# Decay factors of a gated linear attention by in-place products instead of summed logarithms, gates and angles with tokens on the partitions

## The chip, the cores and the metric

The kernel runs on one core of a Trainium2 chip. TensorE (PE) multiplies matrices, VectorE (DVE) and ScalarE (ACT) work element by element, GpSimd (POOL) does little here, and SyncE (SP) issues the loads. Each engine works through its own instructions in order. The metric is the device time of one execution in microseconds (us), the median of several runs. Everything is float32; a float32 matmul shows as two PE instructions in the profile, a float32 transpose as one.

## The reference

The first half is a gated linear attention: batch 4, 8 heads, 768 tokens, 48 channels a head, with a complex gate per token and channel. The second half is a mixer over tokens (rank 32) and a two-layer MLP (384 to 1536 to 384).

```python
mag = np.sqrt(a_re * a_re + a_im * a_im)
scale = np.minimum(mag, 0.999) / (mag + 1e-06)
a_re_n, a_im_n = (a_re * scale, a_im * scale)
for t in range(S):
    ar, ai = (a_re_n[:, :, t, :, None], a_im_n[:, :, t, :, None])
    new_re = ar * S_re - ai * S_im
    new_im = ar * S_im + ai * S_re
    kv = np.einsum('bhd,bhe->bhde', k[:, :, t], v[:, :, t])
    S_re, S_im = (new_re + kv, new_im)
    y[:, :, t] = np.einsum('bhd,bhde->bhe', q[:, :, t], S_re)
...
xt = x.transpose(0, 2, 1)          # x: y as (batch, token, head*channel)
h = xt @ U @ V
u = x + h.transpose(0, 2, 1)
ch = np.maximum(u @ w_ch1, 0.0) @ w_ch2
return (u + ch).astype(np.float32)
```

## The kernel before

The 3072 tokens are 24 chunks of 128, six to a batch. Within a chunk, y_t sums q_t k_s times a decay between s and t times the cosine of an angle difference times v_s. Cosine and sine of the summed angles are stacked, so that a head's q and k have 96 rows (48 cosines, 48 sines). The pairs (s, t) of a chunk are cut into seven levels: halves of 64, 32, 16, 8, 4, 2 and 1 tokens, in which s lies in the lower half of a block and t in the upper; one more pass takes s = t.

For each chunk `front_steps` turns q and k to channels on partitions (`turned`, L275) and multiplies them with cosine and sine while they leave PSUM (L277). `decays` sums the logarithms of the gate magnitudes over every token's span by a matmul with a 0/1 matrix of 384 columns, three levels (or suffix and prefix) for one head at a time: 24 such matmuls a chunk (L300), each followed by an exp on ACT into the tile W (L302, shown by the profile as L182, the line of the helper `act`). `weigh` multiplies W by q or k (L311). `own` and `back_steps` then make the products of k and q: 32-token blocks for the inner levels (`blocks`, L286; 32 matmuls a level in four column tiles), merged by masks into the tile DG (L280); `corners` (L364) and `corner` (L356) for the two outer levels. `place` copies DG to the diagonal of AT on POOL (L378). `outputs` multiplies AT by v and adds the carried state G (L393, L395); ACT copies the result, tokens on partitions, to x (L397). `keys` and `state` (L386, L402) carry the state on. Every level has its own factors in W, so no level waits for another.

`gate_steps` makes the logarithms and angles, two chunks at a time, with tokens on partitions; `phase` sums the angles per head by a matmul (L255) with channels on partitions, reduces them (L260 to L264) and takes one sine (L266).

`mixer_steps` works on two chunks of the batch before: `rank`, `mixed`, `uT` (L440, L449, L454), 12 steps of `up` (L462) and two of `down` (L470). In the first five slots DVE also rounds the float64 weights (`single`, L159 to L170).

The program is written slot by slot, one chunk's `back_steps` to a slot; `weave` spreads the steps of the streams of a slot evenly: the next chunk's factors, gates, weights and half a mixer call. The framework then schedules the instructions within each engine's queue. Three mixer calls, for the last batch, stand behind the loop.

## Time and profile before

| | |
|---|---|
| time, median of 3 runs | 1436.69 us (1436.44 to 1446.21) |
| profiled execution, first to last instruction | 1440.2 us |
| PE busy | 1286.4 us, 89% |
| DVE busy | 722.3 us, 50% |
| ACT busy | 728.7 us, 51%, of it 227.1 us in 177 loads of function tables |
| POOL busy | 114.5 us, 8% |

The span and the runs agree within 0.3%. A row of the profile names a line, an engine and an operation, the tiles written and read, the shape (partitions x elements) and the count. PEclk is the granted clock of TensorE as a share of full speed. The x copy of L397 is the last step of a chunk's attention and serves as a milestone.

### The profile page before, as it was taken

Reading aid. Unit: us, or ns where it says so; the run is one execution under the profiler, and the core shown is the slowest. Engines: PE = TensorE matmul, PEld = TensorE weight load, DVE = VectorE, ACT = ScalarE, POOL = GpSimd, SP = SyncE. Lnnn points to the kernel's source line nnn. Section 1 sums busy time; section 2 is a strip of 40 time slices with the busy share of each in tenths; the row PEclk is TensorE's granted clock in tenths of the full one; section 3 lists DMA queues with packets and bytes.
Section 4 is the critical chain, followed back from the end, with each engine's and each line's share of the span. In section 5 each row is a group of like instructions: output and inputs, shape, how many; then the busy total and the mean of one; then the engine's idle time right before and its main releaser. Section 6 shows DMA issues by size and latency. Waiting matters only on the chain. (4 is left out here: it accounts for less than half of the span.)

```text
span 1440.2 us, 33570 instructions
## 1 busy us (share of the span) xinstructions
PE 1286.4 (89%) x15080; PEld 849.6 (59%) x15080; DVE 722.3 (50%) x1359; ACT 728.7 (51%) x1205; POOL 114.5 (8%) x130
## 2 busy tenths in 40 slices
PE   3785878668898999998998998998999999999998
PEld 1452554435576666675565675675566576675666
DVE  3787588585665355455255355355265444420000
ACT  7875337246687167277176267368166263230111
POOL 0003110410001000000001000000000000000000
PEclk9997767688898999999999999999899999999999
DMA  7132223130212102102102102101101100000000
GB/s 147 27 68 56 62 66 92 42 86 10 51 29 46 28 18 47 39 7 46 31 15 46 28 19 46 28 19 24 28 18 24 39 7 2 13 2 11 11 11 11
DMA packets 181103, 50.42 MB, mean 35 GB/s; under 512 B 176416, under 2 KB 176544, under 8 KB 180960
## 3 DMA queue, kind: packets, MB, share of 16 engines
q1 hardware_dynamic: 179424, 43.56, 14.2%
q0 software_dynamic: 1536, 4.72, 0.9%
q8 instruction: 118, 1.93, 0.6%
q14 instruction: 25, 0.20, 0.0%
HBM read 43.55 MB, written 4.72 MB: 34 GB/s over the span
## 5 line engine op out<-in xcount | busy, mean ns | idle before, releaser
L300 PE MATMUL e<-span,lm 128*96 128x384 f32 x1152 | 477.9, 530 | 70.2 <-ACT W L182 52.4
L182 ACT ACTIVATE W<-e 96x384 f32<-96x384 f32 x576 | 272.7, 486 | 303.0 <-PE e L300 248.6
L300 PEld LDWEIGHTS e<-span,lm 128*96 128x96 f32 x1152 | 171.3, 172 | 216.1 <-ACT W L182 141.0
L182 ACT ACT_TABLE_LOAD x177 | 227.1, 1283 | 9.1 <-DMA ar<-in_a_re_dram 4.5
L462 PE MATMUL up<-uT,w 128*128 128x256 f32 x864 | 228.8, 405 | 2.6 <-DVE uT L455 1.9
L311 DVE TENSOR_TENSOR W<-W,kT 96x512 f32<-96x512 f32 x192 | 144.7, 754 | 142.7 <-ACT W L182 142.7
L462 PEld LDWEIGHTS up<-uT,w 128*128 128x128 f32 x864 | 166.8, 200 | 42.3 <-issue 10.8
L470 PE MATMUL down<-w,h 128*128 128x384 f32 x576 | 189.0, 486 | 0.0
L378 POOL COPY AT<-DG 32x256 f32<-32x256 f32 x96 | 98.5, 1026 | 888.9 <-DVE DG L280 884.7
L470 PEld LDWEIGHTS down<-w,h 128*128 128x128 f32 x576 | 109.4, 190 | 75.9 <-issue 2.5
L311 DVE TENSOR_TENSOR W<-W,qT 96x512 f32<-96x512 f32 x192 | 144.9, 755 | 1.5 <-ACT W L182 1.1
L182 ACT ACTIVATE h<-up 128x256 f32<-128x256 f32 x144 | 55.1, 382 | 167.9 <-PE up L462 167.4
L473 DVE TENSOR_TENSOR x<-down,x 128x384 f32<-128x384 f32 x24 | 13.4, 557 | 222.5 <-PE down L470 222.5
L286 PEld LDWEIGHTS inner<-W 96*32 96x32 f32 x7680 | 85.2, 113 | 63.7 <-issue 51.6
L393 PE MATMUL y<-v,AT 128*128 128x48 f32 x384 | 79.9, 306 | 35.2 <-POOL AT L378 35.2
L286 PE MATMUL inner<-W 96*32 96x32 f32 x7680 | 102.0, 202 | 7.9 <-issue 6.6
L393 PEld LDWEIGHTS y<-v,AT 128*128 128x128 f32 x384 | 68.9, 226 | 41.2 <-POOL AT L378 36.7
L260 DVE TENSOR_TENSOR f<-ph,last 96x512 f32<-96x512 f32 x40 | 27.4, 684 | 92.9 <-PE ph L255 87.7
L395 PE MATMUL y<-G,W 96*128 96x48 f32 x320 | 72.8, 315 | 0.0
L280 DVE COPY_PREDICATED DG<-mask,inner 128x256 f32<-128x256 int32 x120 | 52.3, 436 | 23.8 <-PE inner L286 22.7
L395 PEld LDWEIGHTS y<-G,W 96*128 96x128 f32 x320 | 61.1, 234 | 2.7 <-issue 1.8
L255 PE MATMUL ph<-span,th 128*96 128x128 f32 x384 | 54.5, 286 | 6.1 <-DVE f L260 4.7
(86 smaller groups left out, 1103.4 us busy)
## 6 DMA issues: line engine op xcount, KB each, us to landing
q<-in_q_dram SPq DMA_DIRECT2D x48, 192.0 KB, 3.2
k<-in_k_dram SPq DMA_DIRECT2D x48, 192.0 KB, 3.8
raw<-in_moe_w_ch_dram SPq DMA_DIRECT2D x24, 384.0 KB, 3.2
ar<-in_a_re_dram SPq DMA_DIRECT2D x24, 192.0 KB, 3.4
ai<-in_a_im_dram SPq DMA_DIRECT2D x24, 192.0 KB, 3.7
v<-in_v_dram SPq DMA_DIRECT2D x24, 192.0 KB, 2.6
out_dram<-x POOLq DMA_DIRECT2D x24, 192.0 KB, 2.1
span<-in_spans_dram SPq DMA_DIRECT2D x1, 576.0 KB, 5.4
```

The lines of the kernel that those rows point to most:

```text
L182: nc.scalar.activation(out=o, in_=i, func=f, **kw)
L255: nc.tensor.matmul(out=ps[0:D2, j], lhsT=head(th, hh * HH + j), rhs=prefix, start=True, stop=True)
L260: nc.vector.tensor_tensor(out=f, in0=ps[0:D2], in1=T["last", i - 1][:, hs].unsqueeze(2).to_broadcast([D2, HH, CH]), op=OP.add)
L280: nc.vector.copy_predicated(out=DG[i % 2], mask=mask[:, n].unsqueeze(1).to_broadcast([128, H, BLK]), data=ps)
L286: nc.tensor.matmul(out=ps[js, h], lhsT=lhs(h)[:, js], rhs=rhs(h)[:, js], start=True, stop=True, tile_position=(0, j * BLK))
L300: nc.tensor.matmul(out=ps[0:D2].rearrange("p l t -> p (l t)"), lhsT=head(lm, h), rhs=span[:, tri * 3 * CH:(tri + 1) * 3 * CH], start=True, ...
L311: nc.vector.tensor_tensor(out=o, in0=o, in1=f, op=OP.mult)
L378: nc.gpsimd.tensor_copy(out=AT[i % 2][js, :, js], in_=DG[i % 2][js])
L393: nc.tensor.matmul(out=y[:, h], lhsT=AT[i % 2][:, h], rhs=T["v", i][:, h], start=True, stop=(c == 0))
L395: nc.tensor.matmul(out=y[:, h], lhsT=w[:, h], rhs=T["G"][:, h], start=False, stop=True)
L462: nc.tensor.matmul(out=ps, lhsT=w1[:, f, ff * 128:(ff + 1) * 128], rhs=st["uT"][:, f], start=(f == 0), stop=(f == KD - 1))
L470: nc.tensor.matmul(out=ps, lhsT=st["h"][:, ff, cc * CH:(cc + 1) * CH], rhs=w2[:, ff], start=(ff == 0), stop=(ff == KF - 1))
```

## The change

The decays are no longer sums of logarithms. `gate_steps`, now for three chunks at a time, makes the gate magnitude m itself, the decay from each token to its chunk's end (suf, by one matmul of 384 columns a chunk) and cosine and sine, all with tokens on the partitions: the angles are summed by one or two matmuls a chunk (prefix, and tail for the chunk before). `prep_steps` multiplies q and k with cosine and sine, then turns q, k and m to channels on partitions (`turn`: 24 transposes, six ACT copies from PSUM), and forms the products of m over blocks of 2, 4, ... 128 tokens (`totals`, seven products on DVE). `chain_steps` keeps one pair of factors q, k (tile QK) and grows it in place: after the products of a level, `grow` multiplies the upper halves of q by the total of the lower sibling block and the lower halves of k by that of the upper one, one DVE instruction of 1024 elements; then come the products of the next level. So the levels run from the smallest to the largest, one after the other. `place` runs on ACT. `outputs` makes y transposed (v, padded to 64 columns a head, is the stationary operand, two heads beside each other), and `rows_of_y` turns it back through PE. The mixer and the weights are as before. Two requests for function-table sets are added (`preload_act_table_set`).

```diff
+GC = 3
...
-    pa = pool("pa", 2)
+    pa = pool("pa", 1)
+    pg = pool("pg", 2)
...
+    pkc = pool("pkc", 1)
+    pQK = pool("pQK", 2)
+    pT1 = pool("pT1", 1)
...
-    psE = pool("psE", 2, space=PSUM)
+    psT = pool("psT", 2, space=PSUM)
...
+    psY = pool("psY", 2, space=PSUM)
...
+        T["qk", i] = pqk.tile([128, 2, H, D], FP, tag="qk", name="qk")
+        for u, src in enumerate((q, k)):
+            nc.sync.dma_start(out=T["qk", i][:, u], in_=rows(src, i))
+        nc.sync.dma_start(out=VP[i % 3][:, :, 0:D], in_=rows(v, i))
...
+            nc.scalar.preload_act_table_set("natural_log_exp_and_others")
+            x, y, l = st["x"], st["y"], tmp("l")
             act(l, x, AF.Ln)
             act(x, l, AF.Exp, scale=0.5)
+            act(y, x, AF.Ln, bias=eps)
+            T["suf", g] = pg.tile([128, GC, DM], FP, tag="suf", name="suf")
+            n = T["suf", g].rearrange("p c m -> p (c m)")
+            act(n, T["ar", g], AF.Abs)
+            nc.vector.tensor_tensor(out=x, in0=x, in1=n, op=OP.add)
+            nc.vector.scalar_tensor_tensor(out=y, in0=l, scalar=0.5, in1=y, op0=OP.mult, op1=OP.subtract)
             nc.vector.tensor_scalar(out=l, in0=l, scalar1=0.5, scalar2=LNMAX, op0=OP.mult, op1=OP.min)
+            nc.vector.tensor_tensor(out=l, in0=l, in1=y, op=OP.add)
...
+            x, l = st["x"], st["l"]
...
+            T["m", g] = pg.tile([128, GC, H, D], FP, tag="m", name="m")
+            act(T["m", g].rearrange("p c h d -> p (c h d)"), l, AF.Exp)
+            mul(x, x, T["ai", g])
+        def s3(c):
+            ps = psT.tile([128, DM], FP, tag="t", padded_shape=[128, 512], name="sufl")
+            nc.tensor.matmul(out=ps, lhsT=suffix, rhs=st["l"][:, c * DM:(c + 1) * DM], start=True, stop=True)
+            act(T["suf", g][:, c], ps, AF.Exp)
+        def s4():
+            nc.scalar.preload_act_table_set("trig_and_small")
+            x, y = st["x"], st["y"]
             act(x, x, AF.Arctan)
...
+            nc.vector.tensor_scalar(out=y, in0=x, scalar1=-2.0 / math.pi, scalar2=0.5, op0=OP.mult, op1=OP.add)
+            nc.vector.scalar_tensor_tensor(out=y, in0=T["ar", g], scalar=0.0, in1=y, op0=OP.is_lt, op1=OP.mult)
+            nc.vector.scalar_tensor_tensor(out=y, in0=x, scalar=1.0 / math.pi, in1=y, op0=OP.mult, op1=OP.add)
+        def s5(c):
+            f = F[:, c]
+            i = g * GC + c
+            first = where(i)[1] == 0
+            ps = psT.tile([128, DM], FP, tag="t", padded_shape=[128, 512], name="ph")
+            nc.tensor.matmul(out=ps, lhsT=prefix, rhs=st["y"][:, c * DM:(c + 1) * DM], start=True, stop=first)
+            if not first:
+                nc.tensor.matmul(out=ps, lhsT=tail, rhs=F[:, (c - 1) % GC], start=False, stop=True)
+            nc.vector.tensor_scalar(out=f, in0=ps, scalar1=MAGIC, scalar2=MAGIC, op0=OP.add, op1=OP.subtract)
+            nc.vector.tensor_tensor(out=f, in0=ps, in1=f, op=OP.subtract)
+        def s6():
+            T["cs", g] = pg.tile([128, GC, H, 2, D], FP, tag="cs", name="cs")
+            cs = T["cs", g].rearrange("p c h u d -> p (c h) u d")
+            f = F.rearrange("p c m -> p (c m)")
+            act(cs[:, :, 1], heads(f), AF.Sin, scale=2.0 * math.pi)
+            act(st["x"], f, AF.Abs)
+            act(cs[:, :, 0], heads(st["x"]), AF.Sin, scale=-2.0 * math.pi, bias=quarter)
+        return [s0, s1, s2] + [lambda c=c: s3(c) for c in range(GC)], [s4] + [lambda c=c: s5(c) for c in range(GC)] + [s6]
...
+        def rotate():
+            T["qkc", i] = pkc.tile([128, 2, H, 2, D], FP, tag="qkc", name="qkc")
+            for u in range(2):
+                mul(T["qkc", i][:, u], T["qk", i][:, u].unsqueeze(2).to_broadcast([128, H, 2, D]), T["cs", g][:, c])
+        def keys():
+            T["ks", i] = pqk.tile([128, H, 2, D], FP, tag="ks", name="ks")
+            mul(T["ks", i], T["qkc", i][:, 1],
+                T["suf", g][:, c].rearrange("p (h d) -> p h d", d=D).unsqueeze(2).to_broadcast([128, H, 2, D]))
+        def turn(src, dst, hh):
+            ps = psT.tile([128, HH, CH], FP, tag="t", name="tr")
+            for j in range(HH):
+                nc.tensor.transpose(out=ps[0:D2, j], in_=src[:, hh * HH + j].rearrange("p u d -> p (u d)"),
+                                    identity=ident)
+            nc.scalar.copy(out=dst[:, hh * HH:(hh + 1) * HH], in_=ps[0:D2])
+        def turn_m(hh):
+            if hh == 0:
+                T["T", i, 1] = pT1.tile([D2, H, CH], FP, tag="T1", name="T1")
+                T["mm", i] = pT1.tile([128, H, 2, D], FP, tag="mm", name="mm")
+                nc.scalar.copy(out=T["mm", i], in_=T["m", g][:, c].unsqueeze(2).to_broadcast([128, H, 2, D]))
+            turn(T["mm", i], T["T", i, 1], hh)
...
+        def totals():
+            at = 0
+            tt = pQK.tile([D2, H * CH], FP, tag="TT", name="TT")
+            for hf in (1, 2, 4, 8, 16, 32, 64):
+                n = H * CH // (2 * hf)
+                new = tt[:, at:at + n].rearrange("p (h b) -> p h b", h=H)
+                at += n
+                old = T["T", i, hf].rearrange("p h (b u) -> p u h b", u=2)
+                mul(new, old[:, 0], old[:, 1])
+                T["T", i, 2 * hf] = new
+        for hh in range(2):
+            add(turn_m, hh)
+        add(totals)
+        add(rotate)
+        for u in range(2):
...
+                add(turn_qk, u, hh)
+        add(keys)
...
+        def inner(n):
+            ps = psA.tile([128, H, BLK], FP, tag="a", padded_shape=[128, 2 * H, BLK], name="inner")
+                for j in range(CH // BLK):
+                    js = slice(j * BLK, (j + 1) * BLK)
+                    nc.tensor.matmul(out=ps[js, h], lhsT=k_of(h)[:, js], rhs=q_of(h)[:, js], start=True, stop=True,
+                                     tile_position=(0, j * BLK))
+            nc.vector.copy_predicated(out=DG[i % 2], mask=mask[:, n].unsqueeze(1).to_broadcast([128, H, BLK]), data=ps)
+        def first():
+            mul(T["QK", i][:, 0], T["QK", i][:, 0], T["T", i, 1])
+        def grow(hf):
+            a, t = T["QK", i][:, :, :, :], T["T", i, hf]
+            n = H * CH // (2 * hf)
+            qk = bass.AP(tensor=a.tensor, offset=a.offset + hf, ap=[a.ap[0], [H * CH - hf, 2], [2 * hf, n], [1, hf]])
+            tt = bass.AP(tensor=t.tensor, offset=t.offset, ap=[t.ap[0], [1, 2], [2, n], [0, hf]])
+            mul(qk, qk, tt)
+        def whole():
+            a = T["QK", i][:, 0, :, CH // 2:CH]
+            mul(a, a, T["T", i, 64][:, :, 0:1].to_broadcast([D2, H, CH // 2]))
+        def place():
+            for j in range(CH // BLK):
+                js = slice(j * BLK, (j + 1) * BLK)
+                nc.scalar.copy(out=AT[i % 2][js, :, js], in_=DG[i % 2][js])
...
+            y = psY.tile([128, HH, CH], FP, tag="y", name="yT")
+            vv = VP[i % 3]
+            for p in range(HH):
+                for u in range(2):
+                    h = 2 * p + u
+                    nc.tensor.matmul(out=y[u * DP:(u + 1) * DP, p], lhsT=vv[:, h], rhs=AT[i % 2][:, h], start=True,
+                                     stop=(c == 0), tile_position=(0, u * DP))
+                for u in range(2 if c > 0 else 0):
+                    h = 2 * p + u
+                    nc.tensor.matmul(out=y[u * DP:u * DP + D, p], lhsT=T["G"][:, h], rhs=q_of(h), start=False,
+                                     stop=True, tile_position=(0, u * DP))
+            st["y"] = py.tile([128, HH, CH], FP, tag="yT", name="yTs")
+            nc.scalar.copy(out=st["y"], in_=y)
...
+                mul(G, T["G"], T["T", i, CH].to_broadcast([D2, H, D]))
...
+        def rows_of_y():
+            ps = psY.tile([128, HH, CH], FP, tag="y", name="yr")
+            for p in range(HH):
+                nc.tensor.transpose(out=ps[:, p], in_=st["y"][:, p], identity=ident)
+            T["x", i] = px.tile([128, DM], FP, tag="x", name="x")
+            nc.scalar.copy(out=T["x", i].rearrange("p (h d) -> p h d", d=D),
+                           in_=ps.rearrange("p a (u e) -> p (a u) e", u=2)[:, :, 0:D])
+        add(inner, 5)
+        add(first)
+        for n, hf in ((4, 1), (3, 2), (2, 4), (1, 8), (0, 16)):
+            add(inner, n)
+            add(grow, hf)
+        add(place)
+        add(corners)
+        add(grow, 32)
...
+        add(whole)
         add(outputs)
         if c < NCH - 1:
             add(state)
+        add(rows_of_y)
...
-        streams = [(0.0, 0.68, back_steps(i))]
+        streams = [(0.0, 1.0, chain_steps(i))]
...
+            streams.append((0.0, 1.0, prep_steps(i + 1)))
+        g, r = i // GC + 1, i % GC
...
+            if r == 0:
+                now, later = gate_steps(g)
+                streams.append((0.0, 1.0, now))
+            elif r == 1:
+                streams.append((0.0, 1.0, later))
...
+        if r == 1 and g + 1 < NG:
+            load_a(g + 1)
```

What this does to PE's queue, where the loop runs beside the mixer. Before, a stretch of a chunk (e: a decay matmul; inner, corners: levels; up: mixer):

```order
L300 MATMUL e_4082<-span_114,lm_3417 96x384
L286 MATMUL inner_4085<-W_3590 32x32 x32
L300 MATMUL e_4119<-span_114,lm_3417 96x384
L462 MATMUL up_4122<-uT_3634,w1_139 128x256 x3
L300 MATMUL e_4127<-span_114,lm_3417 96x384
L300 MATMUL e_4130<-span_114,lm_3417 96x384
L286 MATMUL inner_4133<-W_3858 32x32 x32
L300 MATMUL e_4167<-span_114,lm_3417 96x384
L275 MATMUL tr_4032<-ident_109,q_3498 96x128 x4
L300 MATMUL e_4170<-span_114,lm_3417 96x384
L286 MATMUL inner_4173<-W_3858 32x32 x6
L275 MATMUL tr_4044<-ident_109,k_3501 96x128 x4
```

Now, a stretch of a chunk's levels (tr from mm: the magnitudes of the chunk after):

```order
L351 MATMUL inner_5727<-QK_5568 32x32 x32
L293 MATMUL tr_5764<-ident_108,mm_5762 96x128 x4
L480 MATMUL up_5770<-uT_5413,w1_142 128x256 x3
L351 MATMUL inner_5781<-QK_5568 32x32 x32
L293 MATMUL tr_5815<-ident_108,mm_5762 96x128 x4
L480 MATMUL up_5821<-uT_5413,w1_142 128x256 x3
L351 MATMUL inner_5827<-QK_5568 32x32 x32
L480 MATMUL up_5870<-uT_5413,w1_142 128x256 x3
L255 MATMUL ph_5875<-y_5367,span_113 128x384
L257 MATMUL ph_5875<-F_123,tail_117 128x384
L351 MATMUL inner_5880<-QK_5568 32x32 x32
L480 MATMUL up_5918<-uT_5413,w1_142 128x256 x3
```

The decay matmuls are gone; between two levels of one chunk stand transposes, mixer steps and angle sums, and each inner row now reads the tile QK that DVE has to multiply after the row before it.

ACT's queue, where the gates of a group begin. Before (W: the exp of a decay; x, y, l: gates; ks: keys):

```order
L387 COPY ks_4350<-ks_4351 128x384
L182 ACTIVATE W_4343<-e_4357 96x3x128
L182 ACT_TABLE_LOAD
L182 ACTIVATE l_5298<-x_5087 128x768
L182 ACT_TABLE_LOAD
L182 ACTIVATE x_5087<-l_5298 128x768
L182 ACTIVATE h_3862<-up_4360 128x256
L182 ACTIVATE W_4343<-e_4365 96x3x128
L387 COPY ks_4350<-ks_4368 128x384
L182 ACTIVATE y_5088<-l_5298,leps_121 128x768
L182 ACTIVATE W_4343<-e_4374 96x3x128
L182 ACTIVATE W_4343<-e_4383 96x3x128
```

Now, in the order of one group's start (cs: sine and cosine of the group before; yTs: a chunk's y):

```order
L190 ACTIVATE x_4124<-ar_3675 128x1152
L190 ACT_TABLE_LOAD
L190 ACTIVATE l_4211<-x_4124 128x1152
L404 COPY yTs_3633<-yT_3616 128x512
L190 ACT_TABLE_LOAD
L190 ACTIVATE x_4124<-l_4211 128x1152
L190 ACT_TABLE_LOAD
L190 ACTIVATE y_4125<-x_4124,eps_119 128x1152
L190 ACTIVATE x_4124<-x_4124 128x1152
L190 ACT_TABLE_LOAD
L190 ACTIVATE x_4124<-x_4124 128x1152
L190 ACTIVATE m_4275<-l_4211 128x1152
```

The gate functions came one by one between the W; now they follow each other, and a chunk's yTs stands among them. The sum x + y waits on DVE for the square, and the gates' multiplication by ai, on DVE ahead of the next chunk's `first`, for the second exp of x. All 16 requested table sets are loaded in the program's first gates (two groups' worth); 55 other loads remain where functions change.

More of the change, by code (lines that the diff above doesn't have):

```diff
@@ L58 @@
     D2 = 2 * D
+    DP = 64
     DM = H * D
@@ L399, in state, with corner @@
-        def state():
-            d = psY.tile([128, H, D], FP, tag="y", padded_shape=[128, H, 64], name="dk")
-            for h in range(H):
-                nc.tensor.matmul(out=d[0:D2, h], lhsT=st["ks"][:, h], rhs=T["v", i][:, h], start=True, stop=True)
+        def corner():
+            ps = psA.tile([128, H, 64], FP, tag="a", name="corner")
+            for h in range(H):
+                nc.tensor.matmul(out=ps[0:64, h], lhsT=k_of(h)[:, 0:64], rhs=q_of(h)[:, 64:128], start=True, stop=True)
+            nc.scalar.copy(out=AT[i % 2][0:64, :, 64:128], in_=ps[0:64])
@@ L477, in mixer_steps @@
             add(rank)
-        for cc in range(GC):
+        for cc in range(MC):
             add(mixed, cc)
```

244 lines of the change are left out of this document (51 added, 193 removed).

## The prediction

> **What bounds the kernel now.** I read the page first, then busy time by stretches, the milestones of ACT, and PE's own timeline.
>
> ```profile
> span 1440.2 us, 33570 instructions
> PE 1286.4 (89%) x15080; PEld 849.6 (59%) x15080; DVE 722.3 (50%) x1359; ACT 728.7 (51%) x1205; POOL 114.5 (8%) x130
> ```
>
> The columns of the next view are the stretch, its length, then busy time (and count) of PE, PE's weight loads, DVE, ACT and POOL, the granted clock, DMA share and GB/s.
>
> ```profile
> 120.00:200.00 80.00, 56.72 (x749) 36.30 (x749) 58.77 (x126) 33.77 (x56) 18.80 (x5) 0.76 0.30 73
> 380.00:700.00 320.00, 304.68 (x3753) 204.09 (x3753) 165.19 (x279) 194.85 (x319) 18.49 (x28) 0.96 0.16 33
> ```
>
> The 89% hide two regimes. From 380 us on PE is busy 95% at clock 0.96: it is the bound. Earlier, where DVE rounds the weights, PE is busy 71% at 0.76, DVE 73%. The copies of x give each chunk's pace:
>
> ```profile
> 89.58 0.48 ACT L397 COPY x<-y 128x384 f32<-128x384 f32 x1
> 334.92 0.47 ACT L397 COPY x<-y 128x384 f32<-128x384 f32 x1
> 416.30 0.49 ACT L397 COPY x<-y 128x384 f32<-128x384 f32 x1
> 1299.82 0.48 ACT L397 COPY x<-y 128x384 f32<-128x384 f32 x1 [4.31 <-PE y L395]
> ```
>
> These are chunks 0, 4, 6 and 23: (334.92 - 89.58)/4 = 61.3 us a chunk early, (1299.82 - 416.30)/17 = 52.0 us beside the mixer. The chain of waits then shows the last batch's mixer alone, from here to the end of the span, 124.0 us:
>
> ```profile
> 1316.20 4.00 PE rank L440 x12
> ```
>
> Why 61.3 early: POOL's copies to AT, and PE waiting for them.
>
> ```profile
> L378 POOL COPY AT<-DG x96: 386/398/16040, 78.9 to 1295.6; 32x256 f32<-32x256 f32 x96
> PE y L393 <- POOL AT L378: 35.2, 5, 13.7
> ```
>
> A copy that takes 398 ns at the median took up to 16 us there.
>
> **PE's work for a chunk, from its timeline** (start to next start; columns: start, length, operation, count).
>
> ```profile
> 699.71 2.27 PE L300 MATMUL e<-span,lm 128*96 128x384 f32 x6
> 701.82 7.90 PE L470 MATMUL down<-w,h 128*128 128x384 f32 x24
> 709.56 0.60 PE L275 MATMUL tr<-ident,q 128*96 128x128 f32 x4
> 710.09 1.15 PE L356 MATMUL corner<-W 96*64 96x64 f32 x16
> 711.16 0.64 PE L275 MATMUL tr<-ident,q 128*96 128x128 f32 x4
> ...
> 731.57 1.11 PE L255 MATMUL ph<-span,th 128*96 128x128 f32 x8
> 732.61 0.76 PE L286 MATMUL inner<-W 96*32 96x32 f32 x64
> 733.30 0.89 PE L300 MATMUL e<-span,lm 128*96 128x384 f32 x2
> 734.03 1.46 PE L462 MATMUL up<-uT,w 128*128 128x256 f32 x6
> 735.32 0.81 PE L300 MATMUL e<-span,lm 128*96 128x384 f32 x2
> ...
> 738.24 1.88 PE L393 MATMUL y<-v,AT 128*128 128x48 f32 x16
> 739.96 0.66 PE L462 MATMUL up<-uT,w 128*128 128x256 f32 x2
> ```
>
> Prices: a 384-column matmul 2.11/3 = 0.70 us; a down 7.74; four transposes 0.53; corner 1.07; four 128-column matmuls 1.04, so 0.26 each; a level 0.69; an up step 1.29; 16 instructions of y 1.72.
>
> The mixer's share of a chunk stays: 6 up (7.7), one down (7.7), one mixed and uT (0.7 + 0.4), a third of half of rank's six matmuls (0.7): 17.3.
>
> Before, a chunk adds 24 decays (16.8), 16 transposes (2.1), 8 angle matmuls (2.1), six levels (4.1), corner and corners (1.5, corners as half a level), y (3.4), turning the keys (0.7, priced as transposes by width) and state (1.7, as half of y): 32.4. Together 49.7 against the 52.0 measured, so these prices miss 5%.
>
> After: no decays; 24 transposes (3.2) and four for y (0.5); levels, corner, corners, state as before (7.3); the sums of gates and angles 2.8 matmuls (2.0); y of 16 matmuls with 128 moving columns instead of 48: 16 x 0.26 = 4.2, or 2.1 if neighbouring column halves overlap as the four column tiles of a level do; I take 4.2, as no row shows two halves. 17.2, with the mixer 34.5; with the 5%, **36.2 us** a chunk of PE work.
>
> **The other engines.**
>
> ```profile
> L182 ACT ACT_TABLE_LOAD x177 | 227.1, 1283 | 9.1 <-DMA ar<-in_a_re_dram 4.5 <-PE e L300 1.5
> L280 DVE COPY_PREDICATED DG<-mask,inner 128x256 f32<-128x256 int32 x120 | 52.3, 436 | 23.8 <-PE inner L286 22.7
> L311 DVE TENSOR_TENSOR W<-W,kT 96x512 f32<-96x512 f32 x168 | 115.5, 689 | 142.7 <-ACT W L182 142.7
> L311 DVE TENSOR_TENSOR W<-W,kT 96x1024 f32<-96x1024 f32 x24 | 29.1, 1214 | 0.0
> L223 DVE TENSOR_TENSOR lm<-l,y 128x1536 f32<-128x1536 f32 x12 | 21.1, 1754 | 50.2 <-PE e L300 48.7 <-ACT y L182 1.6
> L161 DVE SCALAR_TENSOR_TENSOR cx<-raw,cx 128x384 uint32<-128x384 uint32 x24 | 13.1, 548 | 0.0
> L159 DVE TENSOR_SCALAR cx<-raw 128x384 uint32<-128x384 uint32 x24 | 8.4, 350 | 5.0 <-DMA raw<-in_moe_w_ch_dram 5.0
> L357 ACT COPY AT<-corner 64x512 f32<-64x512 f32 x24 | 13.9, 578 | 71.1 <-PE corner L356 71.1
> L367 ACT COPY AT<-corners 32x256 f32<-32x256 f32 x48 | 17.3, 360 | 19.1 <-PE corners L364 18.8
> L182 ACT ACTIVATE x<-x 128x768 f32<-128x768 f32 x36 | 30.3, 843 | 0.3
> L182 ACT ACTIVATE h<-up 128x256 f32<-128x256 f32 x144 | 55.1, 382 | 167.9 <-PE up L462 167.4
> ```
>
> DVE, a chunk: six masked copies (2.6), `first` and six `grow` of 1024 elements (7 x 1.214 = 8.5), `whole` (0.7), `totals` (0.7 and six shorter ones, 1.5), `rotate` and `keys` (768 elements, between 0.689 and 1.214: 3 x 0.95 = 2.9), state (2 x 0.55): 18.0. The strided `grow` has no row; L311's strided rows cost as much as dense ones, so I take no surcharge. Gates: seven products of 1152 (between 0.95 and 1.754: 1.35) and three cheaper ones (0.8) a group of three, and 1.0 a chunk for the angles: 5. Mixer 1.7. So 24.7, under PE's 36.2. The weights add, early, 24 pieces of 5 x 0.548 + 4 x 0.350 = 4.1 us and about four more for U and V: 115 us over five chunks, 23 each.
>
> ACT, a chunk: six `turn` copies (3.5), mm (0.8), `place` and corners (6 x 0.36), corner and yTs (1.2), x and suf (0.9), 13 gate functions of 1152 (1.2, extended from 0.843 at 768) over three chunks (5.2), 55/24 table loads (2.9), six relu (2.3): 19. Neither bounds by its sum. `place` on ACT costs 1.4 us a chunk beside other work, and frees PE of the POOL waits.
>
> **Where the new waits lie.** A level must be followed on DVE by a masked copy and a `grow`, 0.436 + 1.214 = 1.65 us, before PE may start the next. The cover is what stands between two levels in PE's queue: four transposes and an up step, 0.53 + 1.29 = 1.82. If that cover were gone, nine such hand-offs would cost 15 us a chunk. It just holds, but DVE also has 8.9 us of other work of a chunk (totals, rotate, keys, angles, mixer, state) among nine hand-offs, about 1.0 each, of which the level itself hides 0.69: 0.3 late, 2.7 us a chunk (0 to 5).
>
> At a group's start ACT has, from the corner copy on: QK 0.6, three functions 3.6, load and Ln 2.5, yTs 0.6, load and Exp 2.5, load and Ln 2.5, Ln 1.2, load and Exp 2.5: 16 us. DVE waits for that Exp with the product by ai, and behind it in its queue stand x<-down, the masked copy and `first` (3.6 in all with the product): 19.5. PE has the corner copy to wait for (0.6), y (4.2), state (1.7), a down (7.7), yr, a level and transposes with a mixed (3.0): 17.2. So 2.3 us short, and about as much again where `Arctan` is late in the same way: 4.6 a group, 1.5 a chunk (0 to 4).
>
> A gap on PE costs more than itself:
>
> ```profile
> 140.00:150.00 10.00, 2.09 (x10) 2.09 (x11) 6.24 (x15) 0.00 (x0) 7.68 (x4) 0.50 0.01 2
> 150.00:160.00 10.00, 10.00 (x45) 8.52 (x45) 1.15 (x3) 1.35 (x3) 0.00 (x0) 0.50 0.00 1
> ...
> 460.00:470.00 10.00, 10.00 (x39) 8.75 (x40) 0.56 (x1) 6.24 (x9) 0.00 (x0) 0.53 0.01 2
> 470.00:480.00 10.00, 10.00 (x40) 6.40 (x39) 4.26 (x7) 3.32 (x8) 0.00 (x0) 0.79 0.10 20
> ```
>
> From 460 to 480 PE is busy throughout at 0.53 and 0.79: 10 x 0.47 + 10 x 0.21 = 6.8 us lost. I take half of it a group, 1.1 a chunk (0 to 2.3). A chunk beside the mixer: 36.2 + 2.7 + 1.5 + 1.1 = **41.5 us**, bounds 36.2 to 47.5.
>
> The Trainium skill ("ScalarE: Activation LUTs", What ACT_TABLE_LOAD costs) says that a switch of table sets costs about 1.28 us and a drain of 1.38 besides. Here it does not:
>
> ```profile
> 13.59 1.28 ACT L182 ACT_TABLE_LOAD   x1
> 14.88 0.84 ACT L182 ACTIVATE y<-y 128x768 f32<-128x768 f32 x1
> ```
>
> The next function starts 1.29 us after the load. By the page the ACT chain above, with its four loads, would be 5.5 us longer, 1.8 a chunk, and the sum 31 us higher; the trace leaves this no chance of its own, and I keep 1.283.
>
> **The sum.** Chunk 0's x: three chunks' gates instead of two, and 16 requested table loads (20.5 us) of which some eleven fall into the first gates; the removed loads and the single `cs` pass win part back: 100 us (90 to 115) against 89.6. Chunks 1 to 4: DVE 18 + 5 + 23 = 46 us, nearly without the POOL stalls; 49 each (43 to 58), 196. Chunk 5, with neither weights nor mixer: 17.2 of PE work at the early clock of 0.76 (23) and seven hand-offs on DVE (12): 35. Chunk 6: 41.5. Then 17 x 41.5 = 705.5 and the mixer alone, 125 with the x copy. 100 + 196 + 35 + 41.5 + 705.5 + 125 = 1203 us against 1440.2. The median stands 0.2% under the profiled span: **1200 us**.
>
> **The rivals.**
> - *PE wall to wall*: all hand-offs hidden, 36.5 us a chunk: 1200 - 18 x 5 = 1110. For it: before, PE reached 95% busy. Against: there no level waited for another. Chance 0.15.
> - *DVE and PE in series*: DVE's 24.7 us and, end to end, what it waits for (nine PE pieces of 0.7 to 1.1 us, 8; at groups 16 us of ACT chain against some 5 of own work, 4 a chunk; y's end and yr, 10 with the mixer's down between): 47 us, 1200 + 18 x 5.5 = 1300. For it: one queue, no spare factors. Chance 0.15.
> - *Slower, by the clock*: short gaps before every level keep PE at the low clock of the early stretch, or below, and all 36.2 us grow with it. Break-even is (1440 - 1203)/18 = 13.2 more, 54.7 a chunk, of it 4.2 waits: 36.2/50.5, a clock of 0.72. At 0.6 it is 64.5 and 1615. For it: 0.76 at 71% busy, and 0.50 for a whole busy stretch (150 to 160). Against: those stretches hold waits of ten microseconds; here PE would be busy about 87%. Chance 0.06. The skill's page "TensorE: Matmul & The Clock Gate" (Part 1: The HAM clock gate) says that about 3.4 us of sustained work restore the full clock; the row at 150 to 160 differs.
> - *The table requests do nothing*: they stand at the queue's start, and 55 loads remain; this is in the sum.
>
> **How the numbers follow.** My case (39 to 45 us a chunk) has 0.64. Likeliest time 1200. The range takes in the rivals on the fast and the serial side and the early bounds (chunks 0 to 4 alone -34 to +51): 1110 to 1320. Faster by over 1% (what can be told from no change): 0.64 + 0.15 + 0.15 less 0.02, 0.92; within 1%: 0.02; slower: 0.06.
>
> **What would show it.** x copies 41.5 us apart from chunk 7 on, chunk 6's near 372; inner rows on PE waiting for DVE's QK about 3 us a chunk; one PE gap of 3 to 7 us a group, behind ACT's gates; DVE about 700 busy, ACT about 490 with 71 loads; clock above 0.9 from 370 us on. Wrong if the clock there is under 0.8, if `grow` takes more than 1.4 us, or if ACT's turn copies hold PE's transposes.

## The result, and the profile after

The changed kernel takes 1037.62 us (median of 4 runs, 1035.16 to 1040.24) against 1440.88 us beside it: a ratio of 0.7208, 95% interval 0.7175 to 0.724. It is faster, and by far more than forecast: 1200 us was expected, and the time lies below the low end of the range, 1110.

From the page of the profiled execution after the change: span, busy time by engine, and PE's granted clock in 40 equal slices of the span (each digit in tenths):

```profile
span 1033.4 us, 30196 instructions
PE 867.1 (84%) x13808; PEld 623.3 (60%) x13808; DVE 635.1 (61%) x1103; ACT 466.9 (45%) x731; POOL 17.5 (2%) x37
...
PEclk9966755567769989999999899999999999989999
```

PE lost 419 us of busy time and is still the busiest engine. ACT and DVE lost 262 and 87. The copies of x, here of chunks 0, 4, 6, 7, 8 and 23, on ACT's timeline (start, length, operation):

```profile
93.15 0.48 ACT L424 COPY x<-yr 128x384 f32<-128x384 f32 x1 [3.01 <-PE yr L422]
259.46 0.46 ACT L424 COPY x<-yr 128x384 f32<-128x384 f32 x1
320.91 0.48 ACT L424 COPY x<-yr 128x384 f32<-128x384 f32 x1 [1.35 <-PE yr L422]
365.35 0.46 ACT L424 COPY x<-yr 128x384 f32<-128x384 f32 x1
396.13 0.48 ACT L424 COPY x<-yr 128x384 f32<-128x384 f32 x1 [1.35 <-PE yr L422]
909.43 0.48 ACT L424 COPY x<-yr 128x384 f32<-128x384 f32 x1 [6.43 <-PE yr L422]
```

Cut at these copies, the stretches of the changed kernel (stretch, length, busy time and count of PE, PE's weight loads, DVE, ACT and POOL, granted clock, DMA share, GB/s):

```profile
0.00:93.15 93.15, 38.43 (x596) 25.55 (x600) 66.11 (x148) 78.08 (x81) 4.37 (x13) 0.84 0.40 82
93.15:259.46 166.31, 99.83 (x2090) 74.33 (x2090) 157.35 (x331) 65.01 (x94) 0.00 (x0) 0.62 0.28 73
259.46:293.74 34.28, 19.48 (x558) 15.83 (x558) 28.78 (x40) 23.72 (x30) 0.00 (x0) 0.70 0.27 54
293.74:320.91 27.17, 26.51 (x416) 18.71 (x420) 17.23 (x27) 11.00 (x26) 0.00 (x0) 0.81 0.19 39
320.91:909.43 588.52, 570.78 (x9767) 411.98 (x9767) 355.52 (x543) 274.37 (x465) 9.31 (x17) 0.98 0.12 28
909.43:1033.40 123.97, 112.11 (x402) 76.94 (x401) 10.16 (x19) 14.74 (x38) 3.78 (x7) 0.94 0.03 12
```

The same two main stretches of the kernel before:

```profile
89.58:334.92 245.34, 177.47 (x2290) 115.42 (x2290) 178.41 (x394) 117.83 (x183) 49.10 (x16) 0.75 0.25 63
416.30:1299.82 883.52, 850.39 (x10548) 568.34 (x10547) 418.26 (x710) 466.51 (x800) 50.09 (x84) 0.97 0.12 25
```

| stretch, us | before | forecast | after | missed by |
|---|---|---|---|---|
| to chunk 0's x | 89.6 | 100 | 93.2 | -7 |
| chunks 1 to 4 | 245.3 | 196 | 166.3 | -30 |
| chunk 5 | 46.9 | 35 | 34.3 | -1 |
| chunk 6 | 34.5 | 41.5 | 27.2 | -14 |
| chunks 7 to 23 | 883.5 | 705.5 | 588.5 | -117 |
| the rest | 140.4 | 125 | 124.0 | -1 |
| span | 1440.2 | 1203 | 1033.4 | -170 |

Two regimes remain. From chunk 7 on PE is busy 97% at clock 0.98: of 34.6 us a chunk it works 33.6 and is idle for 1.0 (before: 50.0 and 1.95 of 52.0). From chunk 1 to 4 DVE is busy 95%, and PE 60% at clock 0.62. What PE waits for in the later stretch, in the view of waits (us in total, times, longest):

```profile
PE inner L351 <- DVE QK L193: 12.9, 13, 2.2
```

The waits for DVE's QK, in which the forecast's hand-offs and group starts would show, come to 12.9 us in 17 chunks, 0.8 each.

### The profile page after: what moved, and what is told of

Read it like the earlier page. It is cut to its first block, busy times and chain, and to the rows that moved or that the text cites. A ratio compares the mean times of both kernels' runs of the same rounds, so it can differ in the third digit from the quotient of the medians.

```text
span 1033.4 us, 30196 instructions
## 1 busy us (share of the span) xinstructions
PE 867.1 (84%) x13808; PEld 623.3 (60%) x13808; DVE 635.1 (61%) x1103; ACT 466.9 (45%) x731; POOL 17.5 (2%) x37
## 4 chain that ended last, share of the span: by engine, by line
PE 66%; DVE 18%; ACT 12%; issue 3%; DMA 1%; POOL 0%; DVEq 0%; ACTq 0%
PE up L480 17%; PE down L488 16%; PE inner L351 7%; PE tr L293 6%; DVE QK L193 5%; ACT L190 3%; PE dk L409 3%; PE corner L388 3%; PE yT L397 3%; ACT x L190 2%; PE yT L401 2%; PE ph L255 2%; DVE DG L353 1%; PE sufl L238 1%; PE uT L472 1%
## 5 line engine op out<-in xcount | busy, mean ns | idle before, releaser
L351 PE MATMUL inner<-QK 96*32 96x32 f32 x9216 | 128.0, 208 | 68.6 <-DVE QK L193 62.3
L351 PEld LDWEIGHTS inner<-QK 96*32 96x32 f32 x9216 | 107.9, 119 | 125.8 <-issue 67.3
L193 DVE TENSOR_TENSOR QK<-QK,TT 96x1024 f32<-96x1024 f32 x144 | 162.3, 1127 | 33.1 <-PE corner L388 20.1
L295 ACT COPY QK<-tr 96x512 f32<-96x512 f32 x96 | 55.3, 579 | 79.5 <-PE tr L293 78.3
L293 PE MATMUL tr<-ident,qkc 128*96 128x128 f32 x384 | 72.2, 321 | 11.8 <-DVE qkc L193 9.5
L293 PEld LDWEIGHTS tr<-ident,qkc 128*96 128x96 f32 x384 | 49.5, 147 | 30.6 <-issue 10.1
L193 DVE TENSOR_TENSOR QK<-QK,T 96x1024 f32<-96x1024 f32 x48 | 58.3, 1215 | 0.0
L193 DVE TENSOR_TENSOR qkc<-qk,cs 128x768 f32<-128x768 f32 x48 | 44.2, 952 | 12.6 <-ACT cs L190 12.0
L374 ACT COPY AT<-DG 32x256 f32<-32x256 f32 x96 | 38.5, 401 | 13.8 <-DVE DG L353 12.8
L397 PE MATMUL yT<-AT,VP 128*64 128x128 f32 x384 | 40.9, 306 | 1.5 <-ACT AT L389 1.3
```

What stands on the lines that cost most here:

```text
L193: nc.vector.tensor_tensor(out=o, in0=a, in1=b, op=OP.mult)
L293: nc.tensor.transpose(out=ps[0:D2, j], in_=src[:, hh * HH + j].rearrange("p u d -> p (u d)"), identity=ident)
L295: nc.scalar.copy(out=dst[:, hh * HH:(hh + 1) * HH], in_=ps[0:D2])
L351: nc.tensor.matmul(out=ps[js, h], lhsT=k_of(h)[:, js], rhs=q_of(h)[:, js], start=True, stop=True, tile_position=(0, j * BLK))
L374: nc.scalar.copy(out=AT[i % 2][js, :, js], in_=DG[i % 2][js])
L397: nc.tensor.matmul(out=y[u * DP:(u + 1) * DP, p], lhsT=vv[:, h], rhs=AT[i % 2][:, h], start=True, stop=(c == 0), tile_position=(0, u * DP))
```

## The experiments

Two theories stood against each other. *Wall to wall*: beside the mixer PE is the bound before and after, so removed PE work goes off one to one, and the new hand-offs hide under the mixer and the transposes; early, DVE's sum is the bound. *Hand-offs*: a level waits for the masked copy and the `grow` of the level before, and the loop carries a part of that, as the forecast had it. Times in these sections are medians of runs beside the kernel before; paces are from one profiled execution each.

### The removed sums alone

Eight of the 24 products that sum over spans are left out of the kernel before; ACT's work stays.

```
 def decays(i, tri, h):
...
+    if tri == 2:
+        act(T["W", i, tri][:, :, h], span[0:D2, 0:3 * CH]..., AF.Exp)
+        return
     ps = psE.tile(...)
     nc.tensor.matmul(...)
```

> The kernel before, with the sums over spans of the last three of the nine levels left out (8 of the 24 384-column products of a chunk; ScalarE takes exp of a constant instead, the same instructions), so these three levels' decays are not the reference's. If TensorE is the bound of its loop, what is removed goes off one to one: 8 x 0.70 = 5.6 us, from 52.0 to 46.4 a chunk in chunks 7 to 23, 18 chunks 101 us; in chunks 1 to 5, with TensorE busy 72%, 0 to 5 each: 1340 to 1320. If ScalarE's exps and the waits between the engines carry the loop, it falls by 0 to 3 a chunk: 1390 to 1440.

1337.11 us against 1440.57, ratio 0.9276 (0.9234 to 0.9318). The stretch from chunk 6's x to chunk 23's:

```profile
403.82:1199.91 796.09, 759.14 (x10258) 529.03 (x10257) 419.99 (x711) 471.88 (x814) 51.54 (x84) 0.97 0.13 28
```

46.8 us a chunk, 5.1 less, for 5.4 us less of PE work (759.14 against 850.39 over 17). ACT had as much to do as ever. That is 0.67 a product, near the price of 0.70, and it goes off the time nearly one to one: the loop before was PE's.

### The hand-offs, taken away and doubled

The five `grow` between the inner levels left out (the sixth, `grow` of 32, stays):

```
 def grow(hf):
+    if hf < 32:
+        return
```

> The changed kernel without the five `grow` products of a chunk: the factors are left as they are between the levels, so what the levels compute is not the reference's; every other instruction stays. VectorE falls by 6.1 us a chunk, and a level waits for no product. Theory A (TensorE wall to wall in the loop, VectorE the bound in chunks 1 to 4): the loop stays at 34.6 us a chunk, or falls by at most the 0.8 that TensorE waits there for VectorE's products; chunks 0 to 4 fall by about 5 each; 1037 - 25 = 1012, or 1000 with the 0.8. Theory B (hand-offs carry a part of the loop): the loop falls by 2 to 5 us a chunk, 920 to 975.

And `grow` done twice, the second time by ones. The edit stands in `grow` itself and so doubles all six of a chunk, not the five that the expectation counts:

```
+    ones = singles.tile([128, 1], FP, name="ones")
+    nc.vector.memset(ones, 1.0)
...
     mul(qk, qk, tt)
+    mul(qk, qk, bass.AP(tensor=ones.tensor, offset=ones.offset,
+                        ap=[[ones.ap[0][0], D2], [0, 2], [0, n], [0, hf]]))
```

> The changed kernel, with each of the five `grow` products of a chunk done twice on VectorE, the second time by ones. The loop (chunks 7 to 23, 34.6 us each) has VectorE busy 355.5 of 588.5 us, 20.9 a chunk; five more products of 1.215 us make it 27.0. Theory A (TensorE works wall to wall, and the hand-offs to VectorE are hidden with room to spare): the loop stays at 34.6 to 36 us a chunk; chunks 1 to 4, where VectorE is busy 95%, go from 41.6 to about 47.5; in all some +30 us, 1068. Theory B (my forecast's: a level follows masked copy and `grow` with a cover that just holds): the cover of 1.82 us is passed by about 1 us at five levels a chunk, 5 more in the loop, 1037 + 30 + 18 x 5 = 1157.

Without it 984.6 us (ratio 0.6844, 0.6802 to 0.6885), doubled 1113.09 (0.7736, 0.7702 to 0.777). Chunks 1 to 4, then 7 to 23, first without:

```profile
85.98:232.50 146.52, 88.41 (x2140) 66.97 (x2139) 132.69 (x306) 64.90 (x95) 0.00 (x0) 0.72 0.33 83
284.24:862.20 577.96, 565.78 (x9701) 413.79 (x9700) 261.75 (x455) 271.13 (x466) 9.32 (x17) 0.98 0.13 28
```

and doubled:

```profile
102.32:293.22 190.90, 100.73 (x2102) 76.58 (x2105) 180.65 (x345) 65.55 (x94) 0.00 (x0) 0.62 0.24 59
367.17:989.07 621.90, 580.65 (x9710) 421.23 (x9708) 471.21 (x645) 273.73 (x463) 9.85 (x18) 0.95 0.12 26
```

In the loop, taking 5.5 us a chunk off DVE gains 0.6 (34.0 against 34.6): that is all that these five `grow` cost. Adding 6.8 costs 2.0, of it 1.4 as idle time of PE and 0.6 as more busy time, with the clock at 0.95: the cover has room, but not for twice the work. The wall-to-wall theory is right as the kernel stands; its guess for the doubling was 0 to 1.4 a chunk, and the other theory's 5. Both whole times, though, fall between the two theories' forecasts, mostly because the early chunks were mispriced.

In chunks 1 to 4 the time follows DVE: 24.7 us less work, 19.8 less time; 23.3 more work, 24.6 more time. The 25 us expected for chunks 0 to 4 without `grow` were 27; chunk 5, 24.5 instead of 34.3, came on top, and so the whole went below the 1000 expected. Of the 78 us that the doubling added to the span, 46 arose up to chunk 6, where 30 had been expected, and 33 in the loop (the mixer alone took 2 less).

### The products of y

They form y transposed, each with 64 or 48 output rows, so that two neighbours lie in different column halves of the array. First the same products in another order:

```
-    for p in range(HH):
-        for u in range(2):
+    for u in range(2):
+        for p in range(HH):
...
```

> The changed kernel with the products of y in another order: first all of the lower column half (u = 0), then all of the upper, so that neighbours share a half. If neighbouring halves run beside each other (the 32 instructions of y took 1.91 us, and I had priced 4.2), y takes 3.5 to 4.2 us a chunk, TensorE's work grows by 1.6 to 2.3, and where TensorE is the bound (18 chunks) the time grows by 29 to 41: 1070. If a 128-column product of 64 columns is that short by itself, nothing changes: 1037.

1064.67 us, ratio 0.7397 (0.736 to 0.7435). PE's timeline, the changed kernel first (32 instructions of y, then dk and the transposes back):

```profile
601.47 0.44 PE L397 MATMUL yT<-AT,VP 128*64 128x128 f32 x4 [0.16 <-ACT AT L389]
...
603.38 1.56 PE L409 MATMUL dk<-VP,ks 128*96 128x48 f32 x16
604.78 0.62 PE L422 MATMUL yr<-ident,yTs 128*128 128x128 f32 x4
605.33 0.39 PE L351 MATMUL inner<-QK 96*32 96x32 f32 x22
```

and then the reordered one, also 32 instructions:

```profile
616.35 0.43 PE L397 MATMUL yT<-AT,VP 128*64 128x128 f32 x2 [0.16 <-ACT AT L389]
...
619.62 1.56 PE L408 MATMUL dk<-VP,ks 128*96 128x48 f32 x16
```

1.91 us against 3.27 from the first of y to dk. So neighbouring halves do run beside each other: a pair takes about 0.22 us, and one product alone 0.20. The new order also puts a head's second product right behind its first, into the same output; that is not the reason. In the first chunk of a batch there is no second product, and the eight that are left take 1.02 us in the changed kernel and 1.51 in this order (from 527.83 and from 540.23 on). The loop takes 36.2 us a chunk, 1.6 more, and PE's busy time 1.5 more. The Trainium skill ("TensorE: Matmul & The Clock Gate", Part 3: Packing small matmuls) says that products at different tile positions run concurrently; this pair of rows agrees, with 1.91 against 3.27.

Then y in token layout, as before the change:

```
-    y = psY.tile([128, HH, CH], ..., name="yT")
...
+    y = psY.tile([128, H, D], ..., name="y")
+    for h in range(H):
+        nc.tensor.matmul(out=y[:, h], lhsT=AT[i % 2][:, h], rhs=VP[i % 3][:, h, 0:D], ...)
+        if c > 0:
+            nc.tensor.matmul(out=y[:, h], lhsT=q_of(h), rhs=T["G"][:, h], ...)
...
-    add(rows_of_y)
```

> The changed kernel with y in token layout, as before the change: 16 products with 48 moving columns, no transposes of y, x copied straight from it. From the rows: y 3.4 us a chunk (32 instructions, 1.72 per 16) against 1.91 and 0.55 for the transposes. If TensorE is the bound, +0.95 us in 18 chunks and something early, 1037 + 17 = 1054 to 1060; if the way from AT over yT and its copies to x decides, the shorter way is faster: 1020 to 1030.

1084.97 us, ratio 0.7554 (0.7508 to 0.7601): the sign as expected from the rows, the size not (1054 to 1060). Its timeline and its stretch:

```profile
663.07 0.32 PE L394 MATMUL y<-VP,AT 128*128 128x48 f32 x2
...
666.58 0.88 PE L473 MATMUL down<-w,h 128*128 128x384 f32 x2
```

```profile
336.88:955.90 619.02, 603.17 (x9672) 450.26 (x9672) 353.97 (x543) 264.96 (x448) 9.86 (x18) 0.95 0.12 27
```

y takes 3.51 here, near its price, and 1.05 more than 1.91 and 0.55 for the transposes. The loop takes 1.8 more a chunk, with PE busy 1.9 more. Most of the rest lies in the `up` steps (busy 169.9 us in the stretch against 159.1) and the state's products (26.2 against 21.9), while the downs took no longer (148.1 against 150.6). So the granted clock, 0.95 on the mean, does not explain it as a loss of 3% throughout, and the cause stays open. Chunks 1 to 4 lost 14 us besides (45.1 a chunk), not by more work on DVE (155.0 us against 157.4): DVE waited longer, above all for the loads of the weights (8.1 us against 1.5). Why these came later was not tried.

### The early stage

The copies of `place` on ACT in the kernel before:

```
-    nc.gpsimd.tensor_copy(out=AT[i % 2][js, :, js], in_=DG[i % 2][js])
+    nc.scalar.copy(out=AT[i % 2][js, :, js], in_=DG[i % 2][js])
```

> The kernel before, with the four copies of `place` on ScalarE instead of GpSimd. In chunks 1 to 4 TensorE waited 34.7 us for GpSimd's copies: these go, and the pace falls from 61.3 towards VectorE's 178/4 = 44.6, or ScalarE's and TensorE's own: 1440 - 35 = 1405 (1380 to 1420). The loop keeps 52.0 a chunk. If the copies were late only because something else was, 1435 to 1440.

1408.23 us, ratio 0.9762 (0.9713 to 0.9811), as expected. By stretches, chunks 1 to 4, 5 and 6, and 7 to 23:

```profile
90.81:286.66 195.85, 160.91 (x2278) 101.33 (x2275) 177.57 (x392) 120.48 (x195) 0.00 (x0) 0.83 0.32 79
286.66:376.48 89.82, 79.46 (x1108) 48.15 (x1109) 58.16 (x106) 63.43 (x103) 0.00 (x0) 0.85 0.16 32
376.48:1267.01 890.53, 852.56 (x10552) 567.34 (x10551) 414.21 (x710) 492.84 (x870) 8.78 (x16) 0.98 0.12 25
```

Chunks 1 to 4 gained 49.5 us; chunks 5 and 6 gave 8.4 back and the loop 7.0.

Then the other way round, GpSimd's copies in the changed kernel, once where `place` now stands and once right before y:

```
-    nc.scalar.copy(out=AT[i % 2][js, :, js], in_=DG[i % 2][js])
+    nc.gpsimd.tensor_copy(out=AT[i % 2][js, :, js], in_=DG[i % 2][js])
```

> The changed kernel, with the four copies of `place` back on GpSimd. VectorE is busy 95% in chunks 1 to 4, and GpSimd's copies took up to 16 us there before: chunks 1 to 4 rise from 41.6 to 50 or more, 1037 + 35 to 70 = 1072 to 1107; the loop stays at 34.6. If the moving of `place` had no share in the early gain: 1037 to 1042.

```
-    add(place)
     add(corners)
     add(grow, 32)
     add(corner)
     add(whole)
+    add(place)
     add(outputs)
```

> The changed kernel with the four copies of `place` on GpSimd and moved to stand right before y, as in the kernel before; on GpSimd where the change put them they cost 4 us in all. If it is their place, ahead of corners, `grow`, corner and `whole`, that hides them, TensorE waits for them in chunks 1 to 4 as before (34.7 us over four chunks before; -12 a chunk when ScalarE took them), and the time is 1042 + 20 to 45 = 1062 to 1087. If GpSimd copies are simply no longer starved: 1042 to 1050.

1042.14 us (0.7221, 0.7171 to 0.7272) and 1053.39 (0.7309, 0.7286 to 0.7332). In both, the first case written down missed: on GpSimd at its new place the copies cost 4.5 us, within the intervals nothing, where I had expected 35 or more; right before y they cost 16, between the two cases written down (5 to 13, and 25 to 50). The groups of GpSimd's copies in chunks 1 to 4 (busy us, mean ns), in the kernel before, then in the changed kernel at the new place, then right before y:

```profile
L378 POOL COPY AT<-DG 32x256 f32<-32x256 f32 x16 | 49.1, 3069 | 193.2 <-DVE DG L280 192.5
```

```profile
L374 POOL COPY AT<-DG 32x256 f32<-32x256 f32 x16 | 25.8, 1610 | 142.9 <-DVE DG L353 142.2
```

```profile
L374 POOL COPY AT<-DG 32x256 f32<-32x256 f32 x16 | 34.5, 2153 | 142.6 <-DVE DG L353 141.9
```

And PE's waits for them in the same chunks, in the kernel before, at the new place and then right before y:

```profile
PE y L393 <- POOL AT L378: 34.7, 4, 13.7
```

```profile
PE yT L397 <- POOL AT L374: 3.6, 1, 3.6
```

```profile
PE yT L397 <- POOL AT L374: 10.9, 2, 5.4
```

The copies are slow in all three, but y waits for them 3.6 and 10.9 us, against 34.7 in the kernel before. So two things in the change took the stall away, and a move to another engine was needed for neither: `place` now has corners, a `grow`, corner and `whole` between itself and y, and the copies are shorter beside the new DVE work. Why they are shorter was not settled.

The table requests left out:

```
-    nc.scalar.preload_act_table_set("natural_log_exp_and_others")
...
-    nc.scalar.preload_act_table_set("trig_and_small")
```

> The changed kernel without its requests for tables. All 16 requested loads stand in ScalarE's first 42 us (16 x 1.283 = 20.5), and 55 loads remain in any case. If the requests do nothing but delay the first gates, chunk 0's x comes at 75 to 80 instead of 93, and the time falls by 13 to 18: 1022. If they keep a set in place, the loads of the functions rise above 55 and the time stays or grows.

1037.11 us, ratio 0.7188 (0.7144 to 0.7233): no change. Its loads, and its first stretches:

```profile
L190 ACT ACT_TABLE_LOAD x57 | 73.1, 1283 | 6.4 <-DMA ar<-in_a_re_dram 5.4
```

```profile
0.00:85.95 85.95, 38.85 (x596) 25.53 (x600) 59.26 (x133) 59.90 (x67) 4.37 (x13) 0.83 0.36 72
85.95:259.47 173.52, 100.59 (x2090) 75.07 (x2090) 163.58 (x345) 64.84 (x95) 0.00 (x0) 0.63 0.31 78
```

57 loads instead of 71: the requests save two of the functions' own loads, 55 against 57. Chunk 0's x comes 7 us earlier, half of what I expected (the first 5.4 us pass in waiting for the first input anyway). But chunk 4's x comes at 259.47, as before at 259.46: DVE has 222.8 us to do up to there (223.5 with the requests), and an early start of chunk 1 only leaves it more to do behind it.

Last, the weights' rounding spread over six slots, and in two kernels also begun between the first gates' steps, without the requests (12 pieces there, or 8):

```
-    each = -(-len(weights) // (NCH - 1))
+    each = -(-len(weights) // NCH)
...
-    if i < NCH - 1:
+    if i < NCH:
```

> The changed kernel with the weights' 32 pieces rounded in six chunks' slots (0 to 5) instead of five, 6 a slot instead of 7. If VectorE's sum bounds the early stage (busy 157 of 166 us in chunks 1 to 4, and chunk 4 ended at 259.5 us with and without the table requests), each of slots 0 to 4 loses a piece of 4.1 us and chunk 5, with 28.8 of 34.3 us busy, takes two: -20 + 6 = -14, 1023 (1018 to 1030). If TensorE at its early clock of 0.62 or the hand-offs bound it, nothing: 1037.

```
...
+    n0 = 12
+    weave((0.0, 1.0, g0 + g1 + [lambda: load_a(1)] + prep_steps(0)), (0.0, 1.0, weights[:n0]))
+    weights = weights[n0:]
+    at = [len(weights) * n // NCH for n in range(NCH + 1)]
```

> The changed kernel without table requests, with the first 12 of the weights' pieces (U, V, a third of w1) rounded between the first gates' steps, and the other 20 over six slots. VectorE was idle 27 of the first 86 us without the requests; if its sum bounds the early stage, filling these takes up to 25 us off the end of chunk 5, and the spreading is in it: 1010 to 1018. If the pieces delay the first gates as long as they take (30 us), chunk 0's x moves from 86 to 105 or more and the gain is that of spreading alone: 1023 to 1030.

> As the one before, with the first 8 pieces (U and V, the small ones) between the first gates' steps and 24 over six slots, four each (16.4 us of VectorE). The same theory gives less delay of the first gates and three more microseconds in each slot: 1012 to 1022.

1032.92 (ratio 0.7176, 0.7163 to 0.719), 1031.82 (0.7172, 0.7161 to 0.7184) and 1033.88 us (0.718, 0.7164 to 0.7196). All three lie 4 to 6 us below the changed kernel, but the intervals overlap its own; a better version is not shown, and all three forecasts (1023, 1010 to 1018, 1012 to 1022) missed. The variant with 12 pieces, chunks 1 to 4, 5 and 6, and 7 to 23:

```profile
103.13:247.09 143.96, 95.25 (x2090) 69.59 (x2090) 127.44 (x247) 64.88 (x94) 0.00 (x0) 0.69 0.28 66
247.09:318.30 71.21, 50.73 (x1030) 37.75 (x1031) 60.62 (x104) 35.74 (x55) 0.00 (x0) 0.66 0.27 59
318.30:905.89 587.59, 568.96 (x9701) 411.14 (x9700) 353.69 (x540) 273.20 (x465) 9.31 (x17) 0.98 0.13 27
```

Chunk 4 is done 12 us sooner, and chunk 6 only 2.6: chunks 5 and 6 take 71.2 us instead of 61.5, with PE busy 71% at clock 0.66. So DVE's sum sets the pace of chunks 1 to 4, but emptying it there does not carry through to the loop. Chunk 6 alone takes 38.2 us instead of 27.2: at one place, before a sum of the gates (sufl), PE waits 6.4 us for ACT. The rest of what holds chunks 5 and 6 was not taken apart.

## Why the prediction was wrong

The bound was named rightly and the mechanism of the gain too: the removed sums go off PE's time one to one. The mechanism of the likeliest case was not: it put 5.3 us of waits a chunk beside PE's work, and the rival with PE wall to wall, given 0.15, is what happened. Even that rival's 1110 was too slow. By steps:

- **PE's work, 36.2 us: measured 33.6.** The term that was mis-sized is y: I took 4.2, though the text named 2.1 if halves overlap. It is 1.91, and reordering it cost 1.6 a chunk. With 1.9 the sum is 32.2, and 33.6 is 4% above: the 5% on top came out about right, but partly by luck. In the kernel before most of the 2.3 us that it stood for was idle time (1.95), not work, and in the changed kernel's stretch 18 downs fall where 17 were priced.
- **Hand-offs, 2.7: measured 0.3, or 0.8 with the group starts.** The step that failed is the margin: a cover of 1.82 between two levels against 1.65 of DVE work, with the rest of DVE's work on top. From the masked copy to the end of `grow` it is 1.56 us in the changed kernel (609.18 to 610.74):

```profile
609.18 0.44 DVE L353 COPY_PREDICATED DG<-mask,inner 128x256 f32<-128x256 int32 x1 [0.85 <-PE inner L351]
609.52 1.22 DVE L193 TENSOR_TENSOR QK<-QK,T 96x1024 f32<-96x1024 f32 x1
```

  The cover of 1.82 is near the low end of what PE has there, not the typical. In the 119 gaps between two levels of a chunk, read off PE's timeline, stand about 2.1 us of other work on the mean. Here it is 2.5, transposes, an `up` step and a sum of the gates:

```profile
611.00 0.76 PE L351 MATMUL inner<-QK 96*32 96x32 f32 x64
...
614.20 0.99 PE L351 MATMUL inner<-QK 96*32 96x32 f32 x64
```

  And I had spread 8.9 us of other DVE work evenly over nine hand-offs. Of DVE's other work, gates included, about a third (4.0 of 11.0 us a chunk) starts between corner and the next chunk's first level, where PE has y, the state and downs.
- **Group starts, 1.5: measured 0.5.** The waits do lie where they were put: four times PE waits 1.7 to 2.2 us before a level, 7.8 in all, where a sum or product of the gates stands on DVE ahead of the masked copy. I had doubled a wait of 2.3 us by a second one.
- **The clock, 1.1: some 0.7, and already counted.** A gap did cost more than itself. PE's timeline around the longest wait, and the stretch around a wait of 1.7 us at 576.6:

```profile
477.45 2.75 PE L488 MATMUL down<-w,h 128*128 128x384 f32 x8
482.41 0.75 PE L351 MATMUL inner<-QK 96*32 96x32 f32 x64 [2.21 <-DVE QK L193]
483.09 4.54 PE L488 MATMUL down<-w,h 128*128 128x384 f32 x8
```

```profile
570.00:600.00 30.00, 28.11 (x517) 20.47 (x516) 25.74 (x35) 16.23 (x27) 0.54 (x1) 0.89 0.25 53
```

  Eight instructions of `down` take 2.75 us ahead of the wait and 4.54 behind it. Over the whole loop the clock is 0.98, so this is some 0.7 us a chunk (an estimate, 2% of 34.6). But it lies in the 33.6 of work, and the loss at a clock of 0.97 in the kernel before lay in the 52.0 from which the 5% was taken. I added it once more on top.
- **Chunks 1 to 4, 49 each: measured 41.6.** DVE was the bound, as said, and 95% busy, but with 39.3 us a chunk instead of 46. The instructions were counted rightly; their durations may not be added. DVE's timeline in the changed kernel (start, length):

```profile
156.81 0.36 DVE L167 TENSOR_SCALAR cx<-raw 128x384 uint32<-128x384 uint32 x1
157.08 0.56 DVE L175 TENSOR_TENSOR w<-w,cx 128x384 f32<-128x384 f32 x1
157.55 0.36 DVE L177 TENSOR_SCALAR cy<-raw 128x384 uint32<-128x384 uint32 x1
157.82 0.56 DVE L169 SCALAR_TENSOR_TENSOR cx<-raw,cx 128x384 uint32<-128x384 uint32 x1
```

  Each starts 0.09 us before the recorded end of the one ahead. Over the 331 instructions of these chunks that is 30 us, 7 a chunk, about the whole error. The same 0.09 between masked copy and `grow` makes the hand-off's 1.65 us 1.56.
- **Chunk 6, 41.5: measured 27.2.** It was priced as a mean chunk, but the mixer gives its slots two different halves, the first without any down. The copies of x after it show long and short in turn: 44.4 us to chunk 7's, 30.8 to chunk 8's. The kernel before had the same (34.5 for chunk 6 against a mean of 52.0), and I read past it.
- **Chunk 0, chunk 5, the rest:** 100, 35 and 125 against 93.2, 34.3 and 124.0. The requested loads did fall into the first gates, all 16 of them, but leaving them out brought chunk 0's x only 7 us forward, and the end did not depend on it.
- **The range.** Each bound was carried alone. With y at 2.1 and all three waits at their zero ends a chunk is 34.0 by my own prices, 7.5 less in 18 chunks, and the early bound takes off 34 more: 1203 - 135 - 34 = 1034. The measured time is close to that sum of good ends, and that it fits so well is partly chance: the early gain came from DVE's overlapping instructions, and 14 us of the loop's from a short chunk 6, neither of them from the cover. The three waits were not independent, though: hand-offs and group starts hide under the same other work of PE.
- **The other rivals.** DVE and PE in series fell with the doubled `grow` (2.0 us for 6.8 more), and the slower case with the clock of 0.98. That the table requests do nothing to the time is confirmed.

## What to carry to other kernels

Before a new dependence is priced as a wait, take from the order what stands between the two ends of it on the engine that waits, place by place; where that engine has independent work in its queue at each of them, as the mixer's here, hand-offs of 1.6 us are covered almost entirely, and the loop's time is the sum of the engine's own work. Add up starts, not durations, where a trace's instructions overlap. And when several unknowns depend on the same cover, carry them to the end of the range together. A loss that the calibrating run had too, like the clock's here, must not be added a second time.

## What the runs showed of the hardware

- A float32 product with 48 moving columns and 128 output rows took about as long as one with 128 moving columns and 64 or 48 output rows: 3.51 us for 16 of the one, 3.27 for 16 of the other, 0.20 to 0.22 each. Between these two kinds the width of what moves did not set the price; two of the second kind in different halves took about 0.22 together.
- DVE's instructions overlap by about 0.09 us in the records where one follows another without a wait. The Trainium skill ("VectorE: DVE Perf Modes", The DRAIN you can't avoid) has the next instruction wait until the pipe is empty, and starts of instructions that are not held come earlier; the rows from 156.81 on show the earlier start, 0.27 and 0.47 us after instructions of 0.36 and 0.56.
- GpSimd's copy of 32x256 elements, 0.39 us at its shortest, took 1.6 to 3.1 us on the mean while DVE was over 70% busy, in three kernels.
- PE at 60% busy time ran at a granted clock of 0.62 over 166 us, and at 97% at 0.98; without `grow` it was 0.72 in these chunks, at the same 60%. Beside the mixer, waits of only 1.7 to 2.2 us were followed by slower work: 0.89 over 30 us around one of them.
